# Splitting the stationary side of a Linformer-attention and hard-swish kernel into 64- and 32-column tiles

## Chip, cores, metric

One Trainium2 chip, one NeuronCore. The metric is the device time of one execution in microseconds (us); lower is better. L12 is a line of the kernel that a profile is of, so the same statement has other line numbers in the changed kernels (the layers: L497 and L532 before, L172 after).

## The reference

Attention with keys and values projected from 1024 to 64 positions, for 8 batches of 8 heads, then two layers with a hard-swish between:

```python
k_proj = np.einsum('ks,bhsd->bhkd', E, k)           # E, F: 64 x 1024
v_proj = np.einsum('ks,bhsd->bhkd', F, v)
scores = scale * np.matmul(q, k_proj.transpose(0, 1, 3, 2))
attn   = softmax(scores)
x      = np.matmul(attn, v_proj)                    # then to 8192 tokens x 512
h      = x @ w_in                                   # 512 x 2048
out    = (h * np.clip(h + 3.0, 0.0, 6.0) / 6.0) @ w_out
```

## The kernel before

Everything on TensorE is bf16 with f32 sums in PSUM. The layers of one batch run while the next batch's attention is slipped in between groups of them. Cut to what the change and the argument touch:

```python
def busy(n):                                        # warm-up of TensorE
    ps = pmm()
    for _ in range(n):
        nc.tensor.matmul(ps, ones[:, :P], ones, start=True, stop=True)
busy(12)
# ... projections: keys in columns 0..63, values in 64..127 (L195)
for so in range(SO):
    for e in range(2):
        nc.tensor.matmul(ps[e * KP:(e + 1) * KP], ef_t[e][:, so, :],
                         kqv[self.b]["kv"[e]][:, :, so, :], ...)
# ... then, for the batch after the next:
def turn(self):
    nc.sync.dma_start_transpose(self.kT, ...)       # keys turned by DMA
    ...
    qT_dma[self.b] = q_transposed(self.b)           # queries turned by DMA (batches 2 and 3: elsewhere)
    nc.gpsimd.tensor_copy(mark, last)               # waits for the last one turned
    load_kqv(self.b + 1, ...)                       # then the next batch's loads
# ... scores (L226), values (L244): 64 rows x 64 columns; sums (L264): 128 rows x 32 columns
# ... first layer (L497)
for ko in kos:
    nc.tensor.matmul(h_ps, w_in_sb[:, ko, fo * P:(fo + 1) * P], xT[:, ko, t, :], ...)
# ... second layer (L532)
for fo in range(FO):
    nc.tensor.matmul(o_ps, g[:, fo, c * P:(c + 1) * P], w_out_sb[:, fo, :], ...)
```

The chain in `turn`: the projection's keys go to SBUF, DMA turns them (kT), DMA turns the queries (qT), a one-element copy on GpSimd ("mark") waits for the last of these, and only then are the loads of the batch after issued, which the next projection needs. The queries of batches 2 and 3 are turned elsewhere; there "mark" waits for the keys.

The softmax here doesn't subtract the row's maximum and nothing guards it: scores larger than these inputs give would overflow.

Of the kernel before, what the change touches and what calls it, by code (L numbers as in the profile page):

```python
# [15 lines left out]
def kernel(  # L16
# [11 lines left out]
    nc = tc.nc  # L28
    B, H, S, D = q.shape
    KP = E.shape[0]  # L30
# [3 lines left out]
    P = 128  # L34
    SO = S // P
    KO = d_model // P
    FO = d_ff // P
# [28 lines left out]
    def pmm():  # L66
        return ps_mm.tile([P, TOK], f32, tag="mm", name="mm")

    def pat():
        return ps_at.tile([P, TOK], f32, tag="at", name="at")  # L70


    def g_tile():
        return gpool.tile([P, FO, TOK], bf16, tag="g", name="g")
# [12 lines left out]
    ident = consts.tile([P, P], bf16, name="ident")  # L87
# [9 lines left out]
    def raw_tile(name):  # L97
        return kqv_pool.tile([P, H, SO, D], bf16, tag=name, name=name)


    kqv = {0: {n: raw_tile(n) for n in ("k", "q", "v")}}
    q0 = kqv[0]["q"].rearrange("p h s d -> p (h s d)").rearrange(
        "p (t h s d) -> p t h s d", t=NB, h=H, s=SB)
# [22 lines left out]
    w_in_sb = consts.tile([P, KO, d_ff], bf16, name="w_in_sb")  # L126
    w_out_sb = consts.tile([P, FO, d_model], bf16, name="w_out_sb")
# [7 lines left out]
    for i in range(SB):  # L135
        c = slice(i * FO // SB, (i + 1) * FO // SB)
# [17 lines left out]
    ef_t = [e_t, f_t[:, :, 0, :]]  # L154
    busy(2)

    def q_transposed(b):

        t = qT_pool.tile([P, KO, 2, TOK], bf16, tag="qT", name="qT")
        nc.sync.dma_start_transpose(t.rearrange("p j a (m n) -> p (j a m) n", n=P),  # L160
                                    kqv[b]["q"].rearrange("p h s d -> p (h s d)"))
        return t

    qT_dma = {}

    def rec_tile():
        return att.tile([P, 2, TOK], f32, tag="rec", name="rec", bufs=4)

# [13 lines left out]
    class Attention:  # L182
# [8 lines left out]
        def project(self, alloc):  # L191
            ps = self.ps = alloc()
            for so in range(SO):
                for e in range(2):
                    nc.tensor.matmul(ps[e * KP:(e + 1) * KP], ef_t[e][:, so, :],  # L195
                                     kqv[self.b]["kv"[e]][:, :, so, :],
                                     start=(so == 0), stop=(so == SO - 1))

        def keys_out(self):
            for a in range(2):  # L200
# [116 lines left out]
        def visit(self, n, following):  # L317
# [3 lines left out]
            if n == 1:  # L321
                den, av = self.sums(0, pmm, pmm), self.values(0, pat, pat)
                last = self.scores(3, pat, pat)
                rec = rec_tile()
                inverse(rec, den)
                self.exps(3, last)
                return lambda: self.scaled(0, av, rec)
# [27 lines left out]
    class First:  # L355
# [31 lines left out]
        def queries(self, t, js):  # L387

            ps = pat().bitcast(bf16)[:, :len(js) * TOK]
            for i, j in enumerate(js):  # L390
                for a in range(2):
                    for m in range(2):
                        o = i * TOK + a * HT + m * P
                        nc.tensor.transpose(ps[:, o:o + P],  # L394
                                            q0[:, t, 2 * j + a, 2 * m:2 * m + 2, :].rearrange("p s d -> p (s d)"),
                                            ident)
            q = rec_tile().rearrange("p i n -> p (i n)").bitcast(bf16)[:, :2 * TOK]
            nc.vector.tensor_copy(q[:, :len(js) * TOK], ps)
            for i, j in enumerate(js):
                self.qT[t, j] = q[:, i * TOK:(i + 1) * TOK].rearrange("p (a n) -> p a n", a=2)  # L400
# [93 lines left out]

    def h_part(h_ps, xT, t, fo, kos):
        for ko in kos:
            nc.tensor.matmul(h_ps, w_in_sb[:, ko, fo * P:(fo + 1) * P], xT[:, ko, t, :],  # L497
                             start=(ko == 0), stop=(ko == KO - 1))

    def h_out(h_ps, g, fo):  # L500
        r = rpool.tile([P, TOK], f32, tag="r", name="r")
# [3 lines left out]
    def first_group(xT, t, g, fo):  # L505
        h_ps = pmm()
        h_part(h_ps, xT, t, fo, range(KO))
        h_out(h_ps, g, fo)

    def out_rows(b, t, c):  # L510
        return out_v[b, :, SB * t + 2 * (c % 2) + c // 2, :]


    def second_group(b, t, g, c, copy=None):
        o_dst = out_rows(b, t, c)
        if (b, t, c) == (B - 1, NB - 1, SB - 1):

            most = d_model * 3 // 4
            for piece, copy, dma in ((slice(0, most), nc.vector.tensor_copy, nc.sync),
                                     (slice(most, d_model), nc.scalar.copy, nc.scalar)):  # L520
                n = piece.stop - piece.start
                o_ps = pmm()[:, :n]
                for fo in range(FO):
                    nc.tensor.matmul(o_ps, g[:, fo, c * P:(c + 1) * P], w_out_sb[:, fo, piece],  # L524
                                     start=(fo == 0), stop=(fo == FO - 1))
                o_sb = opool.tile([P, d_model], f32, tag="o_sb", name="o_sb")[:, :n]
                copy(o_sb, o_ps)
                dma.dma_start(out=o_dst[:, piece], in_=o_sb)
            return
        o_ps = pmm()  # L530
        for fo in range(FO):
            nc.tensor.matmul(o_ps, g[:, fo, c * P:(c + 1) * P], w_out_sb[:, fo, :],  # L532
                             start=(fo == 0), stop=(fo == FO - 1))
            if fo % SB == SB - 1:
                yield
        o_sb = opool.tile([P, d_model], f32, tag="o_sb", name="o_sb")
        (copy or nc.scalar.copy)(o_sb, o_ps)  # L537
        nc.sync.dma_start(out=o_dst, in_=o_sb)

    def whole(gen):  # L540
        for _ in gen:
            pass

    def x_tile():
        return xpool.tile([P, KO, NB, TOK], bf16, tag="xT", name="xT")


    xT = x_tile()
    first = First(xT)
    g = [g_tile(), g_tile()]  # L550
# [41 lines left out]
    def pop():  # L592
        if later:
            later.pop(0)()
# [25 lines left out]
    xT = x_next  # L620
# [2 lines left out]

    second = Attention(2)
    for b in range(1, B):
        if b + 1 < B:
            x_next = second.xT = x_tile()
        third = Attention(b + 2) if b + 2 < B else None


        def visits(b, n):
            def nothing():
                pass

            if b == 1:
                n -= SB
                if n < 3:
                    return lambda: second.visit(n, third), nothing
                return nothing, lambda: second.visit(n, third)()
            if b + 1 < B:  # L640
                six = (pmm, pmm), (pat, pat), (pat, pat)
                if (b, n) == (2, 0):
                    return lambda: second.some_scores((2, 0, 1), six), nothing
                if (b, n) == (2, 1):
                    return lambda: second.some_scores((3,), six[1:2]), nothing
                if (b, n) == (2, 3):
                    return lambda: third.projected(pmm), nothing
                if n == 0:
                    return nothing, lambda: second.some_scores(
                        (1, 2, 3), ((pmm, pmm), (pat, pat), (pat, pmm)), third)  # L650
                if n == 2:
                    return second.sums_and_values, nothing
                if n == 5:
                    return second.first_products, nothing
                if n == 6:
                    return lambda: second.last_values(third), nothing
            return nothing, nothing

        for t in range(NB):
            if b == 1 and t == 1:  # L660
                qT_dma[3] = q_transposed(3)
            g = g_tile()
            for fo in range(FO):
                if b < 3 and t == 0 and fo < 2:

                    if fo == 0:
                        TwoGroups(xT, t, g).parts((0, 1, 2), (3,))
                else:
                    first_group(xT, t, g, fo)
                pop()  # L670
                if b == 1 and t == 0 and fo == 10:
                    second.projected()
                if not behind or fo % SB < SB - 1:
                    continue
                inside, after = visits(b, t * SB + fo // SB)
                rows = second_group(*behind[0], fo // SB, nc.vector.tensor_copy if b == 1 else None)
                next(rows)
                next(rows)
                rest = inside()
                whole(rows)  # L680
                after()
                if rest:
                    rest()
            behind = [(b, t, g)]
        second, xT = third, x_next
# [32 lines left out]
```

## Time and profile before

| | before |
|---|---|
| time, median of 6 runs | 507.32 us (507.19 to 507.92) |
| profiled span | 505.3 us |
| TensorE busy | 495.5 us (98%) |
| blocks of instructions fetched for TensorE | 21 |

The row of the instruction queue from the page's part on DMA queues (packets, MB, share of 16 engines):

```profile
q8 instruction: 21, 0.34, 0.3%
```

and two rows of DMA issues (count, median us from issue to landing):

```profile
kT<-kp SPq DMA_TRANSPOSE x7, 2.6
qT<-q SPq DMA_TRANSPOSE x7, 6.7
```

The timeline of before (start, length in us, engine, line) around the end of the chain in `turn`, for batch 3:

```profile
135.79 1.20 SPq L209 DMA_TRANSPOSE kT<-kp  x1
136.72 1.89 PE L532 MATMUL mm<-w_out_sb,g 128*128 128x512 bf16 x8
138.51 0.18 POOL L216 COPY mark<-kT 1x1 bf16<-1x1 bf16 x1 [35.30 <-DMA kT<-kp]
138.54 0.41 PE L226 MATMUL mm<-qT,kT 64*64 64x256 bf16 x8
```

The keys are turned at 138.51 and TensorE uses them at 138.54. TensorE does not wait, but it has next to nothing in hand: any delay of that DMA goes straight into the time.

### The profile page before, as it was taken

How to read it: one execution, taken by the hardware profiler on the slowest of the kernel's cores; microseconds unless marked ns; L12 is line 12 of the kernel's file. 1: busy time of each engine (PE TensorE's matmuls, PEld its weight loads, DVE VectorE, ACT ScalarE, POOL GpSimd, SP SyncE). 2: the span in 40 equal slices, each digit the busy share in tenths (PEclk: the TensorE clock that was granted, in tenths of full speed). 3: DMA queues.
4: the chain of work that ended last, by engine and by line, in shares of the span. 5: the costliest groups of instructions: out<-in, count | busy, mean ns of one | idle time of the engine just before them, and what ended most of it. 6: DMA issues, size and time to landing. Idle time of an engine off the chain costs nothing.

```text
span 505.3 us, 7033 instructions
## 1 busy us (share of the span) xinstructions
PE 495.5 (98%) x2728; PEld 224.9 (45%) x2778; DVE 245.3 (49%) x384; ACT 256.2 (51%) x438; POOL 38.7 (8%) x58
## 2 busy tenths in 40 slices
PE   8899999999999999999999999999999999999997
PEld 4444444444444444444444444444444444444444
DVE  3572736855733573526635455533752446334420
ACT  3757476567574444654555544654455544434431
POOL 8620020010020020010002000000000000000000
PEclk9999999999999999999999999999999999999999
DMA  9999989699199998699217990248110361101112
GB/s 168 198 205 208 195 154 231 123 162 204 61 159 198 260 153 161 137 169 257 98 43 134 215 263 28 62 97 209 42 43 30 82 162 43 40 24 42 43 42 83
DMA packets 78057, 66.02 MB, mean 131 GB/s; under 512 B 36216, under 2 KB 67192, under 8 KB 78024
## 3 DMA queue, kind: packets, MB, share of 16 engines
q0 software_dynamic: 32480, 29.36, 37.1%
q1 hardware_dynamic: 45320, 35.89, 27.1%
q8 instruction: 21, 0.34, 0.3%
q10 hardware_dynamic: 224, 0.33, 0.3%
q14 instruction: 12, 0.10, 0.1%
HBM read 69.73 MB, written 16.94 MB: 172 GB/s over the span
## 4 chain that ended last, share of the span: by engine, by line
PE 97%; ACT 1%; issue 1%; DVE 0%; ACTq 0%
PE mm L532 43%; PE mm L497 43%; PE at L195 2%; PE mm L93 1%; PE at L244 1%; PE at L226 1%; PE mm L244 1%; PE mm L524 1%; PE mm L264 1%; PE at L414 1%; ACT aT L235 0%; PE mm L226 0%; PE at L382 0%; PE at L394 0%; PE mm L195 0%
## 5 line engine op out<-in xcount | busy, mean ns | idle before, releaser
L503 DVE SCALAR_TENSOR_TENSOR g<-r,mm 128x512 bf16<-128x512 f32 x256 | 173.6, 687 | 178.9 <-ACT r L502 178.1
L497 PE MATMUL mm<-xT,w_in_sb 128*128 128x512 bf16 x997 | 229.0, 379 | 1.5
L532 PE MATMUL mm<-w_out_sb,g 128*128 128x512 bf16 x985 | 227.8, 379 | 1.9 <-issue 1.0
L502 ACT ACTIVATE r<-mm 128x512 f32<-128x512 f32 x256 | 152.3, 599 | 74.5 <-PE mm L497 73.2
L497 PEld LDWEIGHTS <-w_in_sb 128*128 128x128 bf16 x1024 | 99.5, 98 | 122.2 <-issue 3.3
L532 PEld LDWEIGHTS <-g 128*128 128x128 bf16 x1008 | 96.7, 98 | 120.6 <-issue 7.4
L537 ACT COPY o_sb<-mm 128x512 f32<-128x512 f32 x55 | 32.3, 587 | 126.6 <-PE mm L532 123.7
L257 DVE TENSOR_TENSOR xT<-at,rec 128x512 bf16<-128x512 f32 x42 | 26.5, 682 | 6.4 <-ACT rec L176 6.4
L235 ACT ACTIVATE aT<-at 128x512 bf16<-128x512 f32 x38 | 20.2, 615 | 9.1 <-PE at L226 9.1
L201 DVE CAST kp<-at 64x512 bf16<-64x512 f32 x12 | 7.7, 677 | 15.5 <-PE at L195 15.5
L216 POOL COPY mark<-qT 1x1 bf16<-1x1 bf16 x4 | 0.7, 176 | 161.9 <-DMA qT<-q 161.9
L235 ACT ACTIVATE aT<-mm 128x512 bf16<-128x512 f32 x18 | 10.3, 613 | 3.6 <-PE mm L226 3.6
L537 DVE COPY o_sb<-mm 128x512 f32<-128x512 f32 x8 | 5.5, 688 | 13.4 <-PE mm L532 13.4
L195 PE MATMUL at<-k,e_t 128*64 128x512 bf16 x48 | 11.5, 382 | 0.0
L195 PE MATMUL at<-v,f_t 128*64 128x512 bf16 x48 | 11.5, 381 | 0.0
L257 DVE TENSOR_TENSOR xT<-mm,rec 128x512 bf16<-128x512 f32 x14 | 9.0, 686 | 4.3 <-PE mm L244 4.3
L176 ACT ACTIVATE rec<-rec 128x1024 f32<-128x1024 f32 x10 | 10.6, 1060 | 0.3
L170 ACT ACTIVATE rec<-mm 128x512 f32<-128x512 f32 x10 | 5.5, 595 | 7.9 <-PE mm L244 5.4
L170 ACT ACTIVATE few<-mm 128x512 f32<-128x512 f32 x10 | 5.4, 595 | 7.4 <-PE mm L264 7.4
L93 PE MATMUL mm<-ones 128*128 128x512 bf16 x18 | 7.4, 549 | 1.5 <-DVE halves L84 1.5
L204 DVE CAST vp<-at 64x512 bf16<-64x512 f32 x12 | 8.3, 694 | 0.4
L195 PEld LDWEIGHTS <-e_t 128*64 128x64 bf16 x56 | 5.6, 109 | 6.2 <-issue 1.9
(75 smaller groups left out, 161.0 us busy)
## 6 DMA issues: line engine op xcount, KB each, us to landing
out_dram<-o_sb SPq DMA_DIRECT2D x63, 256.0 KB, 2.5
rec<-rows SPq DMA_DIRECT2D x40, 256.0 KB, 6.2
k<-in_k_dram POOLq DMA_DIRECT2D x7, 1024.0 KB, 14.1
v<-in_v_dram POOLq DMA_DIRECT2D x7, 1024.0 KB, 20.9
q<-in_q_dram POOLq DMA_DIRECT2D x7, 1024.0 KB, 10.7
w_out_sb<-in_moe_w_out_dram POOLq DMA_DIRECT2D x4, 512.0 KB, 16.3
w_in_sb<-in_moe_w_in_dram POOLq DMA_DIRECT2D x5, 256.0 KB, 9.8
k<-in_k_dram POOLq DMA_DIRECT2D x4, 256.0 KB, 5.6
```

Of the source, the lines that this page charges most:

```text
L93: nc.tensor.matmul(ps, ones[:, :P], ones, start=True, stop=True)
L170: nc.scalar.activation(rec[:, i], den, AF.Ln)
L176: nc.scalar.activation(flat, flat, AF.Exp, scale=-1.0)
L195: nc.tensor.matmul(ps[e * KP:(e + 1) * KP], ef_t[e][:, so, :], kqv[self.b]["kv"[e]][:, :, so, :], start=(so == 0), stop=(so == SO - 1))
L235: nc.scalar.activation(self.aT[j][:, r].rearrange("p a n -> p (a n)"), tiles[r], AF.Exp, scale=scale)
L244: nc.tensor.matmul(tiles[t][c:c + D].rearrange("p (r n) -> p r n", r=2), stationary(r, 2 * j + a), self.aT[j][r:r + KP, :, a, :], start=Tr ...
L257: nc.vector.tensor_mul(self.xT[:, j, t, :], av[t], rec[:, t])
L497: nc.tensor.matmul(h_ps, w_in_sb[:, ko, fo * P:(fo + 1) * P], xT[:, ko, t, :], start=(ko == 0), stop=(ko == KO - 1))
L502: nc.scalar.activation(r, h_ps, AF.Relu, bias=0.5, scale=1.0 / 6.0)
L503: nc.vector.scalar_tensor_tensor(g[:, fo, :], r, 1.0, h_ps, op0=ALU.min, op1=ALU.mult)
L532: nc.tensor.matmul(o_ps, g[:, fo, c * P:(c + 1) * P], w_out_sb[:, fo, :], start=(fo == 0), stop=(fo == FO - 1))
L537: (copy or nc.scalar.copy)(o_sb, o_ps)
```

## The change

The intent: a change of the array's tile shape (rows x columns in use by a matmul) costs TensorE about 0.1 us, as the prediction below reads from the trace, so give the layers, the projections and the transposes the column width of the small attention matmuls beside them: 64 columns at first, 32 (the width of the sums) from batch 2 on. A 128-column matmul becomes two or four that run side by side.

```diff
+    width = [P // 2]
+
+    def in_columns(ps, stationary, moving, **flags):
+        for lo in range(0, stationary.shape[-1], width[0]):
+            nc.tensor.matmul(ps[lo:lo + width[0]], stationary[:, lo:lo + width[0]], moving, **flags)
 ...                                   # projections, both layers, the split last rows, alike:
-            nc.tensor.matmul(h_ps, w_in_sb[:, ko, fo * P:(fo + 1) * P], xT[:, ko, t, :],
-                             start=(ko == 0), stop=(ko == KO - 1))
+            in_columns(h_ps, w_in_sb[:, ko, fo * P:(fo + 1) * P], xT[:, ko, t, :],
+                       start=(ko == 0), stop=(ko == KO - 1))
 ...                                   # transposes of batch 0's second half: two of 64 columns
     for b in range(1, B):
+        if b == 2:
+            width[0] = P // 4
```

More of the change, by code (lines that the diff above doesn't have):

```diff
@@ L194, in project @@
                 for e in range(2):
-                    nc.tensor.matmul(ps[e * KP:(e + 1) * KP], ef_t[e][:, so, :],
-                                     kqv[self.b]["kv"[e]][:, :, so, :],
-                                     start=(so == 0), stop=(so == SO - 1))
+                    in_columns(ps[e * KP:(e + 1) * KP], ef_t[e][:, so, :], kqv[self.b]["kv"[e]][:, :, so, :],
+                               start=(so == 0), stop=(so == SO - 1))
         def keys_out(self):
@@ L393, in queries @@
                         o = i * TOK + a * HT + m * P
-                        nc.tensor.transpose(ps[:, o:o + P],
-                                            q0[:, t, 2 * j + a, 2 * m:2 * m + 2, :].rearrange("p s d -> p (s d)"),
-                                            ident)
+                        n = width[0] if t else P
+                        for lo in range(0, P, n):
+                            nc.tensor.transpose(ps[lo:lo + n, o:o + P],
+                                                q0[:, t, 2 * j + a, 2 * m:2 * m + 2, :].rearrange(
+                                                    "p s d -> p (s d)")[:, lo:lo + n], ident)
             q = rec_tile().rearrange("p i n -> p (i n)").bitcast(bf16)[:, :2 * TOK]
@@ L523, in second_group @@
                 for fo in range(FO):
-                    nc.tensor.matmul(o_ps, g[:, fo, c * P:(c + 1) * P], w_out_sb[:, fo, piece],
-                                     start=(fo == 0), stop=(fo == FO - 1))
+                    in_columns(o_ps, g[:, fo, c * P:(c + 1) * P], w_out_sb[:, fo, piece],
+                               start=(fo == 0), stop=(fo == FO - 1))
                 o_sb = opool.tile([P, d_model], f32, tag="o_sb", name="o_sb")[:, :n]
@@ L531, in second_group @@
         for fo in range(FO):
-            nc.tensor.matmul(o_ps, g[:, fo, c * P:(c + 1) * P], w_out_sb[:, fo, :],
-                             start=(fo == 0), stop=(fo == FO - 1))
+            in_columns(o_ps, g[:, fo, c * P:(c + 1) * P], w_out_sb[:, fo, :],
+                       start=(fo == 0), stop=(fo == FO - 1))
             if fo % SB == SB - 1:
```

## The prediction

> **What bounds the kernel now.** I read the page first, for the share of each engine and the chain that ended last.
>
> ```profile
> PE 495.5 (98%) x2728; PEld 224.9 (45%) x2778; DVE 245.3 (49%) x384; ACT 256.2 (51%) x438; POOL 38.7 (8%) x58
> ...
> PEclk9999999999999999999999999999999999999999
> ...
> PE 97%; ACT 1%; issue 1%; DVE 0%; ACTq 0%
> PE mm L532 43%; PE mm L497 43%; PE at L195 2%; PE mm L93 1%; PE at L244 1%; PE at L226 1%; PE mm L244 1%; PE mm L524 1%; PE mm L264 1%; PE at L414 1%; ACT aT L235 0%; PE mm L226 0%; PE at L382 0%; PE at L394 0%; PE mm L195 0%
> ```
>
> TensorE is busy 98% of the span, the chain is TensorE for 97%, the clock is full everywhere, and VectorE and ScalarE stand at half. Two lines, the two layers (L497 and L532), are 86% of the chain. Busy is not peak, so next came the chain in order of time, where 16 matmuls of a layer always take the same time:
>
> ```profile
> 172.66 3.45 PE mm L497 x16
> ...
> 190.81 3.45 PE mm L532 x16
> ```
>
> 3.45 us / 16 = 216 ns for one 128x512 matmul. The 1024 matmuls of the first layer and the 1024 of the second (16 of them are split 384+128, which comes to the same) need 2048 x 0.216 = 442 us of the 505.3 us span. The view of waits holds only 4.5 us of idle TensorE in six rows, so no wait is there to be removed. What is left is how much a matmul costs beyond 216 ns. That is seen where the tile shape changes, in the timeline of TensorE:
>
> ```profile
> 152.72 1.24 PE L532 MATMUL mm<-w_out_sb,g 128*128 128x512 bf16 x5
> 153.89 0.61 PE L264 MATMUL mm<-aT,halves 128*32 128x512 bf16 x8
> 154.43 0.63 PE L244 MATMUL at<-aT,vp 64*64 64x512 bf16 x8
> 154.99 1.25 PE L532 MATMUL mm<-w_out_sb,g 128*128 128x512 bf16 x5
> ```
>
> The eight sums (128 rows x 32 columns) start at 153.89 and the values at 154.43. Eight 512-column matmuls in 0.54 us: four run side by side, two rounds of 0.216 = 0.43, and 0.11 is left over. The values to the next layer: 0.56 - 0.43 = 0.13 left over. In the trace's records the gap from the last start in one shape to the first in another is 309 to 312 ns wherever the earlier matmul has 512 columns, so 93 to 96 ns more than 216, and the second start after it is late by another 0 (32 columns), 10 (full), 14 (64x64) or 21 ns (128x64). The price is the same if only the columns change (L195 to L497: 311 ns), only the rows (L244 to L195: 306 ns), or both (L264 to L244: 309 ns).
>
> That narrow columns run side by side at full pace is seen at the projections, 64 columns each:
>
> ```profile
> 162.24 0.38 PE L195 MATMUL mm<-k,e_t 128*64 128x512 bf16 x1
> 162.25 0.38 PE L195 MATMUL mm<-v,f_t 128*64 128x512 bf16 x1
> 162.46 0.38 PE L195 MATMUL mm<-k,e_t 128*64 128x512 bf16 x1
> 162.46 0.38 PE L195 MATMUL mm<-v,f_t 128*64 128x512 bf16 x1
> ```
>
> A pair starts within 4 ns, and the next pair 216 ns later: two matmuls in the time of one.
>
> **What the Trainium skill says.** "TensorEngine Tiling (Array Packing)", Key Properties: a change of tiling mode drains TensorE, a change of tile within a mode does not. The trace agrees: about 93 ns at each change, nothing between L244 and L226, both 64x64. The same page, Restrictions: column tiling switches Fast Weight Load off. The trace shows no visible price so far: a load takes 98 ns at 128 columns, 106 to 110 at 64, 92 to 96 at 32, and they overlap. "TensorE: Matmul & The Clock Gate", the section on 56 ns against 53.3: N/2.4 + 2.5 ns per warm matmul (216 measured here at N=512), a floor of about 25 ns from start to start, and about 62 ns per matmul where the sequencer's microcode decodes it. No row of this trace decides which decoding is in force. "Runtime: NRT & Kernel Launch", Instruction fetch mechanics: instructions arrive in blocks of 16 KiB, 256 instructions, while the current ones run. The trace agrees: the instruction queue q8 has 21 packets and 0.34 MB, 16 KB each.
>
> **The change part by part.** No instruction of VectorE, ScalarE, GpSimd or a DMA changes; the order of the programs shows their counts equal. On TensorE a layer's matmul becomes two of 64 columns (batch 0 and 1) or four of 32 (from about 133 us on, some 370 us of the span); the rows of TensorE's program go from 5558 to 16310.
>
> Array time: unchanged. A group of two or four side by side takes 216 ns, as L195 and L264 do.
>
> Changes of shape: I counted them in the order of both programs, with the shapes that the groups by form give. Before: 100, of which 42 into the full shape, 11 into 128x64, 5 into 128x32, 38 into 64x64, the rest into 64x128. After: 87, of which 11 into full, 17 into 128x64, 17 into 128x32, again 38 into 64x64. The projections and the sums no longer stand apart, but scores and values keep 64 rows, so each visit to them still costs two changes. With 103 ns into full (93+10), 114 into 128x64 and 93 into 128x32: before 42x0.103 + 11x0.114 + 5x0.093 = 6.05 us, after 11x0.103 + 17x0.114 + 17x0.093 = 4.65 us. Gain 1.4 us.
>
> Small pieces: at the end, 16 matmuls of 128 columns (56 ns each now, in the records) become 16 groups of four, and their loads have no fast path. By the skill's columns/1.2 GHz the four loads need 4 x 27 = 107 ns if they queue behind each other: an estimate of up to 16 x 51 ns = 0.8 us, at the very end and on the path. The 16 transposes of batch 0's second half become pairs: up to the same again, 0.8 us. Half of each seems likely, because 64-wide loads at L366 already keep 56 ns: 0.8 us together.
>
> Sum: -1.4 + 0.8 = -0.6 us, and the time goes from 507.3 to about 506.7.
>
> **The rivals.** (1) Issue becomes the bound. Four loads and four matmuls in 216 ns allow 27 ns per instruction; today two share 216. For it: the skill's 62 ns under microcode would make a group at least 4 x 62 = 248 ns, some 1650 groups x 32 ns = +53 us, about 560; if the loads cost the same, 496 ns a group, over 960 us. Against: the records show starts 3 to 4 ns apart, and the 24 scores at 321.24 with their 24 loads go through in 0.6 us, 12 ns per instruction, without a hole. But 48 is fewer than the 64 instructions that the skill gives TensorE's queue, so a burst does not prove a sustained rate. I give it 12%.
>
> (2) Instruction fetch. 16310 rows are 64 blocks, one per 32 groups = 6.9 us in the later part against one per some 24 us now. q8's 0.3% of 16 engines x 505 us is 24 us, 1.15 us a block: enough room when nothing is in the way. While the loads of the next batch fill the DMA engines (99% in many slices up to 240 us) a block can start late, and TensorE could starve for some us a few times: +2 to +15 us. I give it 15%.
>
> (3) A gain larger than the count of changes, over 2% = 10 us. It would need 100 changes removed, all there are, or a group faster than 216 ns; nothing in the trace offers either. 1%.
>
> **Range and chances.** The main case, some 75%, lies between 505 and 508.5 (1.4 us of gain, up to 1.6 us of loss at the small pieces, and drift). Fetch stalls stretch it to about 522; issue as the bound lies beyond. The range that should hold 8 in 10 is 504.5 to 525. Faster by over 2% (below 497.2): 0.01. Slower by over 2% (above 517.5): 0.19, the issue rival and a part of the fetch rival. Within: 0.80. Predicted 506.7.
>
> **What would show it.** Right, if in the changed profile 16 groups of four still take 3.45 us in the chain, the gap at changes stays near 310 ns, and layers to sums and to projections have no such gap from batch 2 on. The small pieces at the end then take longer than 16 x 56 ns. Wrong, if groups of four start more than 216 ns apart in a steady stretch (issue), the more so at 32 than at 64 columns; or if idle stretches of a us or more appear on TensorE put down to "issue", thick while DMA is busy and gone after 400 us (fetch); or if rows of TensorE wait for PSUM buffers that were free before.

## The result, and the profile after

| | before | after |
|---|---|---|
| time, median of 6 runs | 507.32 us (507.19 to 507.92) | 508.41 us (507.50 to 509.98) |
| ratio | 1 | 1.0023 (95%: 1.0007 to 1.0039) |
| profiled span | 505.3 us | 507.0 us |
| TensorE matmuls, counted by their weight loads (50 matmul records are missing before) | 2778 | 8154 |
| blocks of instructions | 21 | 63 |

Ratios here and below are the mean time of one kernel's fast runs over that of the other's in the same rounds, so not quite the ratio of the medians. The result lies in the predicted range and within 2%, but on the other side of before than predicted: 1.1 us slower, where 0.6 us faster was expected. The page's rows of the engines and of the instruction queue:

```profile
PE 498.1 (98%) x8154; PEld 249.3 (49%) x8154; DVE 245.2 (48%) x384; ACT 256.4 (51%) x438; POOL 38.7 (8%) x58
...
q8 instruction: 63, 1.03, 0.8%
```

The chain in order of time shows what a group of four now takes:

```profile
219.25 27.74 PE mm L172 x512
```

27.74 us / 128 groups is 217 ns, and in the trace's records the group starts are 216 ns apart, as one full matmul's were. Eight instructions per 216 ns are no strain. The timeline at the sums, which the prediction showed for before:

```profile
153.90 1.90 PE L172 MATMUL mm<-w_out_sb,g 128*32 128x512 bf16 x32
155.63 0.60 PE L271 MATMUL mm<-aT,halves 128*32 128x512 bf16 x8
156.16 0.63 PE L251 MATMUL at<-aT,vp 64*64 64x512 bf16 x8
156.72 1.05 PE L172 MATMUL mm<-w_out_sb,g 128*32 128x512 bf16 x16
```

From the layer to the sums it is 1.73 us = 8 x 0.216: the gap is gone there, and those before and after the values (64x64) are still there. So the intended effect took place. What is new stands in TensorE's waits (total us, times, longest):

```profile
PE mm L233 <- DMA kT<-kp: 1.3, 1, 1.3
PE at L172 <- DMA v<-in_v_dram: 0.9, 2, 0.5
...
PE mm L233 <- DMA qT<-q: 0.2, 1, 0.2
```

Before had no row of TensorE waiting for a DMA. Two more such rows, left out here (batch 0's values 0.6 us, its keys 0.5), lie in the first 20 us, where before waited for other engines instead; the table below starts after them, with a lag of 0.12 us. To see when the time came and went, I paired the 384 instructions of VectorE, which are the same in both kernels, and took how much later each one ends in the changed kernel:

| stretch of the kernel before | lag at its start, us | lag at its end, us | what happens |
|---|---|---|---|
| 54 to 59 | 0.12 | 0.59 | projection waits for batch 1's values; two changes of shape fewer |
| 67 to 76 | 0.58 | 0.79 | scores wait for turned queries |
| 94 to 99 | 0.82 | 0.59 | two changes of shape fewer |
| 136 to 144 | 0.63 | 2.03 | scores wait for turned keys (kT) |
| 144 to 198 | 2.03 | 1.53 | 0.17 back at once, in the scores after the wait (0.78 us in place of 0.98); then three changes of shape fewer |
| 198 to 208 | 1.53 | 2.28 | projection waits for batch 5's values; one change of shape fewer |
| 208 to 502 | 2.28 | 1.71 | six changes of shape fewer |

The losses are 0.5 + 0.2 + 1.4 + 0.75 = 2.8 us, the gains 0.2 + 0.5 + 0.6 = 1.3 us. Of the gains 0.2 us is the time made good right after the keys' wait, whose net cost is so 1.2 us; the other 1.1 us belongs to 11 changes of shape (counted in the order of the weight loads: 100 before, 87 after), 0.1 us each. (The recorded texts speak of batch 4's values at 203 and 204 us; what the turn of batch 4 loads are the values of batch 5.) The largest loss, in the timeline that was shown for before:

```profile
136.43 1.20 SPq L216 DMA_TRANSPOSE kT<-kp  x1
137.35 1.90 PE L172 MATMUL mm<-w_out_sb,g 128*32 128x512 bf16 x32
140.57 0.41 PE L233 MATMUL mm<-qT,kT 64*64 64x256 bf16 x8 [1.31 <-DMA kT<-kp]
140.65 0.18 POOL L223 COPY mark<-kT 1x1 bf16<-1x1 bf16 x1 [36.74 <-DMA kT<-kp]
```

From the issue of the transpose to the first scores: 4.14 us, against 2.75 before. The records of single DMA packets in the trace show why. The transpose's packets run from 137.6 to 138.6, but two of its 32 closing packets of 4 bytes start only at 139.48 and 139.49; at 138.41 a 16 KB packet of the instruction queue starts, and it takes 1.09 us, to 139.50. The trace does not name the engine of a packet; that two packets of 32, one sixteenth, start when the block ends fits one of the 16 engines being held. (The last packet is about 0.9 us late, the scores 1.4 us; "mark" follows the last packet after 1.15 us in place of 0.59, and the records do not show why.) In the kernel before the transpose's last packet starts by 138.0, and the instruction packet comes at 139.37, after it. This gave the theory.

**Theory F**: a block of 256 instructions arrives as one packet of 16 KB, which holds one of the 16 DMA engines for about 1 us. A transfer with packets on that engine ends that much later. Narrow tiles make TensorE's program three times as long (63 blocks in place of 21), so more transfers are hit, and those with no time in hand make TensorE wait. **Rival S**: a moving operand that is read once per column tile slows DMA in SBUF. **Rival C**: chance in DMA times.

### The profile page after: what moved, and what is told of

It reads as the page before. It is cut to its first block, busy times and chain, and to the rows that moved or that the text cites. A ratio compares the mean times of both kernels' runs of the same rounds, so it can differ in the third digit from the quotient of the medians.

```text
span 507.0 us, 17834 instructions
## 1 busy us (share of the span) xinstructions
PE 498.1 (98%) x8154; PEld 249.3 (49%) x8154; DVE 245.2 (48%) x384; ACT 256.4 (51%) x438; POOL 38.7 (8%) x58
## 4 chain that ended last, share of the span: by engine, by line
PE 76%; DMA 18%; POOL 2%; ACT 1%; issue 1%; DVE 1%; SPq 1%; POOLq 0%; ACTq 0%
PE mm L172 71%; DMA q<-in_q_dram 6%; DMA v<-in_v_dram 6%; DMA qT<-q 4%; DMA w_in_sb<-in_moe_w_in_dram 2%; PE at L172 1%; PE at L251 1%; DMA kT<-kp 1%; PE mm L251 1%; PE at L233 1%; POOL q L106 1%; POOL k L110 1%; ACT aT L242 0%; PE mm L271 0%; POOL v L110 0%
## 5 line engine op out<-in xcount | busy, mean ns | idle before, releaser
L172 PE MATMUL mm<-w_out_sb,g 128*32 128x512 bf16 (+3 forms) x3776 | 235.6, 376 | 0.2 <-DVE g L512 0.2
L172 PE MATMUL mm<-xT,w_in_sb 128*32 128x512 bf16 (+1 forms) x3584 | 232.2, 379 | 0.2 <-ACT aT L242 0.2
L172 PEld LDWEIGHTS <-w_in_sb 128*32 128x32 bf16 (+1 forms) x3584 | 112.4, 99 | 108.9 <-issue 1.3
L172 PEld LDWEIGHTS <-g 128*32 128x32 bf16 (+1 forms) x3776 | 110.9, 98 | 110.8 <-issue 7.0
L172 PE MATMUL at<-v,f_t 128*32 128x512 bf16 (+1 forms) x72 | 11.4, 380 | 0.9 <-DMA v<-in_v_dram 0.9
L172 PE MATMUL at<-k,e_t 128*32 128x512 bf16 (+1 forms) x72 | 11.8, 381 | 0.0
L233 PEld LDWEIGHTS <-kT 64*64 64x64 bf16 x224 | 5.6, 106 | 6.2 <-issue 3.2
```

The lines of the kernel that those rows point to most:

```text
L172: nc.tensor.matmul(ps[lo:lo + width[0]], stationary[:, lo:lo + width[0]], moving, **flags)
L233: nc.tensor.matmul(tiles[r][t * KP:(t + 1) * KP, a * HT:(a + 1) * HT], self.kT[r * D:(r + 1) * D, 2 * j + a, :], qT[r * D:(r + 1) * D, j, ...
```

## The experiments

Nine kernels ran, all with correct results, each with five rounds against the kernel before.

**e1, 64 columns to the end.** Half as many extra instructions.

```diff
-        if b == 2:
-            width[0] = P // 4
```

> All tiled matmuls 64 columns wide, to the end. Read from the two profiles: the narrow tiles themselves cost nothing (a group takes 216 ns), the changed kernel gains about 0.1 us at each change of shape that is gone (1.4 us), and loses 2.8 us in four waits of TensorE for DMA (0.5 us at 55.6, 0.2 at 69, 1.4 at 140.6, 0.75 at 204.3). Theory F (instruction blocks): the instruction queue's 16 KB packet holds one DMA engine for about 1 us, and a transfer with packets on that engine ends that much later; with narrow tiles there are 63 such packets in place of 21. Here the program has 9718 rows, 38 blocks, and the changes of shape fall from 100 to 91, worth 0.7 us. The first 133 us are the changed kernel's own, so the waits at 55.6 and 69 should be there again, those at 140.6 and 204.3 may be gone or shorter: time 506.7 to 508, fewer waits than in the changed kernel. Rival S (the array reads the moving operand once per column tile, and that slows DMA in SBUF): half the reads of 32 columns, so waits about half as long everywhere, none gone. Rival C (chance: DMA time varies by run): waits anywhere, times spread like the changed kernel's, 507.5 to 510.

507.17 us (506.90 to 507.92), 0.9996 of before (0.9984 to 1.0008). The waits at 55.6, 140.6 and 204.3 are gone; one of 0.4 us for turned queries is left:

```profile
PE mm L233 <- DMA qT<-q: 0.4, 1, 0.4
```

Two tenths of a us for weights come at 20 as well. This fits F and C. The wait at 55.6 had been expected again, since the program up to there is the changed kernel's own, and it did not come: that one is not tied to the tiles.

**e2, 32 columns from the start.**

```diff
-    width = [P // 2]
+    width = [P // 4]
     ...
-        if b == 2:
-            width[0] = P // 4
```

> All tiled matmuls 32 columns wide from the start; 18262 rows, 71 blocks, changes of shape 86, worth 1.8 us against before. Theory F: blocks come every 6.9 us in the first 133 us too, where the loads of the first batches fill the DMA engines, so new or longer waits for DMA there: the sum of TensorE's waits for DMA 2 to 5 us, time 507.5 to 511, slower than the changed kernel by some 0 to 2 us. Rival S: waits in the first 133 us twice as long as in the changed kernel (0.7 to 1.4 us). Rival C: same as the changed kernel.

508.03 us (507.39 to 510.68), 1.0018 of before (1.0001 to 1.0036); waits of 0.6 us for weights at 20, 0.5 us at the scores at 69 and 0.5 us for the values of batch 5 at 203. Not worse than the changed kernel, so the number of blocks alone does not set the time. On S this run says little: the waits at 20 and 69 add up to 1.1 us, within its 0.7 to 1.4, but the one at 55 is gone.

**e3, the changed kernel with its blocks shifted.** The 12 warm-up matmuls are cut in four: 72 instructions more and the same work, so each block is fetched 72 instructions earlier.

```diff
-    busy(12)
+    busy(12, 4)        # 48 matmuls of 128 columns in place of 12 of 512
```

> The changed kernel with its 12 warm-up matmuls of 512 columns cut into 48 of 128: same time of TensorE while it is waiting for its first data anyway, but 72 instructions more ahead of everything, so every block of 256 instructions is fetched 72 instructions earlier: 1.9 us earlier where tiles have 32 columns, 3.9 us where they have 64. Nothing else changes: the tiles, their reads and their changes of shape are those of the changed kernel. Theory F: the fetch at 138.4 us in the changed profile, which lies on the transpose of the keys (packets 137.6 to 139.5), moves to about 136.5 and leaves it free, so the wait of 1.4 us at 140.6 goes; that at 55.6 is likely to go too (its fetch at 54.9 moves to 51). Time 505.5 to 507, faster than the changed kernel by 1 to 2.5 us and perhaps than the kernel before. Rivals S and C: no change, 507.5 to 510.

508.52 us (508.24 to 511.01), 1.0029 of before (1.0014 to 1.0043). The time is not what F expected, but the named wait is gone:

```profile
137.04 1.90 PE L172 MATMUL mm<-w_out_sb,g 128*32 128x512 bf16 x32
138.87 0.41 PE L233 MATMUL mm<-qT,kT 64*64 64x256 bf16 x8
```

The block is fetched at 135.85, ahead of the transpose's packets, and the scores start 2.76 us after its issue, as in the kernel before. The wait at 69 is gone too, that at 55 was to go and shrank to 0.3 us. The gain was lost again at 203, where the wait for batch 5's values grew:

```profile
PE at L172 <- DMA v<-in_v_dram: 1.2, 1, 1.2
```

That wait ends the chain of `turn`: the transpose of batch 4's queries is issued at 169 us, and the loads follow it. In e3 two blocks fall on that transpose, at 172.6 (a packet of 2.08 us this time) and 178.7. The times of all kernels, the ones below included, put the stretch from the issue of that transpose to the mark that waits for it beside the blocks fetched in it:

| kernel | blocks in the stretch | issue to mark, us | loads of batch 5 end at, us |
|---|---|---|---|
| before | 0 | 8.3 | 198.4 |
| e4, e5, e7 | 0 | 8.8, 8.8, 8.7 | 200.5, 200.9, 199.1 |
| e1, e6, e8, e9 | 1 | 9.3, 9.0, 10.1, 10.1 | 201.2, 200.7, 201.1, 201.6 |
| e2, e3, after | 2 | 10.9, 11.7, 10.9 | 202.6, 203.1, 203.9 |

Against the mean of the four without one (8.65 us), one block goes with 0.3 to 1.4 us more and two with 2.2 to 3.0. The projection wants the values at about 202, so none or one block is covered and two are not. With 32 columns a block is due every 6.9 us (32 groups x 216 ns), shorter than the transpose, so no shift can keep every block out of it. This table alone does not tell F from S: the three kernels with two blocks are also the three with 32 columns at that time. Other transposes do; see the end of this section.

**e4, full tiles up to batch 3, 32 columns from batch 4 on.**

```diff
-    width = [P // 2]
+    width = [P]
-        if b == 2:
+        if b == 4:
     ...
-        for lo in range(0, stationary.shape[-1], width[0]):
+        n = min(width[0], stationary.shape[-1])
+        for lo in range(0, stationary.shape[-1], n):        # and n for width[0] in the slices
```

> Full 128-column tiles up to batch 3's layers, 32 columns from batch 4 on (from about 254 us): the early part, where the loads of the next batch are tight, has the instruction rate of the kernel before. Changes of shape 96, worth 0.5 us. Theory F and theory S both: no waits for DMA in the first 254 us, time 506.6 to 507.0, that is 0.5 us faster than before. Rival C: spread as in the changed kernel. If it is slower than before, the narrow tiles cost something of their own in the steady part that the comparison of the two profiles did not show.

507.88 us (507.56 to 508.71), 1.0009 of before (0.9996 to 1.0022): not the gain that both theories expected. Nor did it run without waits for DMA: batch 1's values cost 0.5 us at 55, with full tiles. The narrow tiles then won back 0.36 us, so that the last copy on VectorE ends only 0.07 us later than before's, but the span is 1.0 us longer. What is lost besides lies after the last copy of ScalarE:

```profile
502.40 0.27 ACT L537 COPY o_sb<-mm 128x128 f32<-128x128 f32 x1 [2.91 <-PE mm L173]
502.70 0.35 ACTq L538 DMA_DIRECT2D out_dram<-o_sb  x1
```

In the packet records the last packets of the two last stores start at 504.56 and 504.76 (in the kernel before, after the same copy at 502.33, at 503.50 and 503.84), and a block of instructions was fetched from 502.65 to 503.71, on top of the stores. F's mechanism at a place that I had not thought of; a mere reading so far, tested by e7.

**e5, the kernel before with 32 instructions more.** Full tiles; the warm-up is cut into 28 shorter matmuls of the same total length.

```diff
-    busy(12)
+    busy(4)
+    busy(4, 2)
+    busy(4, 4)
```

> The kernel before, with full tiles, its 12 warm-up matmuls cut into 28 shorter ones of the same total length: 32 instructions of TensorE more, no work more. The program then ends just past a boundary of 256 instructions, as late32's did (12246 rows, 5590 here: both 42 short of a multiple of 256 in the rows that the listing counts), whose block was fetched at 502.65 to 503.71, on the last stores of the output. Theory F (instruction blocks hold up a DMA engine): a 22nd block is fetched at about 502.6, the last stores land about 0.9 us later, time 508.2, 0.9 us slower than before, though no tile changed. Theory S (the reads of narrow tiles slow DMA) and rival C (chance): no change, 507.2 to 507.6. If the block is not fetched at the end, the run tells nothing on F.

508.46 us (508.39 to 508.70), 1.0021 of before (1.0009 to 1.0034): 0.96 us slower, the size expected, and not where it was expected. The last block was fetched at 499.0 and met nothing. It was the keys' transpose again that was hit:

```profile
136.87 1.89 PE L534 MATMUL mm<-w_out_sb,g 128*128 128x512 bf16 x8
140.14 0.41 PE L228 MATMUL mm<-qT,kT 64*64 64x256 bf16 x8 [1.39 <-DMA kT<-kp]
```

A block is fetched at 138.08 and takes 0.93 us. The transpose's packets, which began at 137.1, end with two stragglers at 139.00 and 139.01, where the block ends, and the scores start 4.21 us after the issue, as in the changed kernel (4.14). So the very wait that cost the changed kernel 1.4 us comes about in the kernel before, without one narrow tile, by moving its block fetches. Rival S cannot do that, and rival C would have to hit all five runs here and spare all five of e6 below.

**e6, the kernel before with 72 instructions more**, the control: `busy(12, 4)` as in e3.

> Control for the two shifts: the kernel before with the warm-up cut into 48 matmuls of 128 columns, 72 instructions more. The last boundary comes 40 instructions earlier than in e5, so its block is fetched about 2 us earlier, ahead of the last stores. Theory F: 507.2 to 507.8, with no wait at the end; a collision elsewhere would show as a wait for DMA beside a fetch. If cutting the warm-up itself costs time, it shows here.

507.43 us (507.33 to 507.51), 1.0000 of before (0.9988 to 1.0013). The block comes at 133.0, well ahead of the transpose, and the scores start 2.75 us after its issue. Cutting the warm-up shows no cost. A wait of about 0.4 us for batch 1's values at 55.3 shows here too, with full tiles: this wait of the changed kernel is not due to the change, or not only.

**e7, e4 with 72 instructions more**: `busy(12, 4)` again.

> late32 (full tiles up to batch 3, 32 columns from batch 4 on) with the warm-up cut into 48, 72 instructions more. In e4 the layers ended only 0.07 us later than in the kernel before and the whole 1.0 us later, because the last block was fetched on top of the last stores. Here that fetch comes about 1 us earlier. Theory F: the end is free again, time 506.8 to 507.2, 0.7 to 1 us faster than e4 and 0.3 to 0.6 faster than before. If the end is late again though the fetch is away from it, F is wrong about the end.

507.10 us (506.73 to 507.58), 0.9994 of before (0.9982 to 1.0007), 0.8 us faster than e4 by the medians; the two ran in different rounds and their intervals overlap, so the profile has to decide. There the last block is fetched at 501.75, about 0.9 us earlier, the last packet of the output starts 1.51 us after the last copy starts, as in before (2.36 in e4), and the span ends no later after the last copies than before's. This run met the wait at 55 as well (0.7 us), and even so is not slower than before.

**e8 and e9, 64 columns at first, 32 from batch 4 or from batch 3 on.** e4 with `width = [P // 2]`, and e9 with `b == 3`.

> 64 columns up to batch 3's layers (e1's, which met one wait of 0.4 us at 68), 32 from batch 4 on; 14198 rows, the last boundary far from the end. Changes of shape 89, worth 1.06 us. Theory F: no wait at 140 or 204 (at most one fetch in the transpose of batch 4's queries, as in e1), no late end: time 506.3 to 507.0, the best of all, if no new collision appears. Theory S: as e1 in the first half, and no more than 0.4 us better than e1.

> e8 with the change to 32 columns one batch earlier, from batch 3 on (about 194 us), after the transpose of batch 4's queries at 168 to 178 is over. Changes of shape 88 in place of 89, worth another 0.15 us; 60 blocks. Theory F: no block in that transpose more than e8 has, so no wait at 204, time 506.2 to 507.0, as e8 or 0.15 us better; if a block now falls on the landing of batch 4's values at about 200, a wait of up to 0.9 us at 204 comes back and the time is 507.0 to 508. Rival S: narrow tiles from 194 on slow the loads of batch 4 that run until 200, wait at 204 as in the changed kernel (0.75 us) whatever the blocks do.

e8: 507.06 us (506.67 to 507.75), 0.9994 of before (0.9980 to 1.0008). e9: 507.00 us (506.71 to 508.12), 0.9996 (0.9983 to 1.0008). Neither has a wait at 140 or 204, though e9's tiles have 32 columns while the loads of batch 5 run until 201.6: against S. Both wait for turned queries at 69, 0.2 and 0.5 us, which their expectations had left out. By the medians these are the fastest, 0.4 us ahead of before (507.42 to 507.50 in these rounds), but the intervals hold 1. No version is shown to be faster than the kernel before; for four with narrow tiles (e1, e7, e8, e9) no loss is shown either.

**All transposes beside the blocks.** The eleven traces hold many more transposes of the same sizes, which separate the width of the tiles from the blocks. From issue to landing (where the view gives no landing, to 0.12 us before "mark"), in us; those of batch 4's queries are in the table above:

| transpose | block starts after its issue by | full tiles | 64 columns | 32 columns |
|---|---|---|---|---|
| keys | no block starts in it | 2.57 to 2.73 (18) | 2.57 to 2.73 (11) | 2.60 to 2.61 (4) |
| keys | 1.98 to 2.15 | 4.16 (e5) | 4.14 (e3, batch 2) | 4.10 (after) |
| queries | no block starts in it | 6.6 to 6.7 (15) | 6.7 (8) | none |
| queries | 0.1 to 1.1 | 6.7 (2) | 6.7 (1) | 6.7 to 7.5 (4) |
| queries | 6.1 to 6.6 | 8.2 to 8.4 (3) | 8.3 to 8.5 (5) | 8.2 to 8.4 (10) |

Those left out have a block elsewhere and lie between these values, except one with two blocks (e2, 9.74). One with 32 columns and a block at 6.12 (e2) took 6.66, so not every late block does harm. Without a block the width makes no difference, while with one at the same place full tiles lose as much as narrow ones: S is out as the cause of these delays, and the place of the block counts, not only its presence. This settles the wait at 69 as well: in the changed kernel, e1, e2, e8 and e9 a block starts 6.2 to 6.6 us after the issue of batch 1's queries and TensorE waits; the other six have no block there and do not, e3 with the changed kernel's own tiles among them.

## Why the prediction was right, and where it was not

- **Array time unchanged at 216 ns a group**: right, for two tiles of 64 columns and for four of 32.
- **Gain of 1.4 us at the changes of shape**: right. The 11 that the table of lags shows by themselves are worth 1.1 us, 0.1 us each, so the 13 some 1.3 (an estimate from these). The gap is a little less uniform than the prediction read it: 306 to 312 ns in before's layers, up to 333 in the work of batch 0, 305 to 320 in the changed kernel. And the six rows of TensorE's idle time, which the prediction put at 4.5 us, add up to 4.1.
- **Small pieces, +0.8 us**: wrong, nothing was lost. In the changed kernel's records the last 16 groups of four matmuls of 128 moving columns start 56 ns apart, as one full matmul did before, and so do the pairs of narrow transposes. The step that failed is the four narrow loads queueing behind each other for 107 ns: the whole group, loads included, took 56 ns.
- **Rival 1, issue**: did not occur, and could be dropped: eight instructions per 216 ns in steady stretches, and eight per 56 ns at the end. That is 14 ns a matmul, below the floor of 25 ns from start to start that the prediction took from the skill.
- **Rival 2, instruction fetch**: the right cause of loss, and the wrong path. I had TensorE starve for instructions; it never did. The blocks delayed other DMAs, and TensorE waited for their data: a term of +2.8 us in the profiled run that the main sum did not have. Of it the 1.4 us for the turned keys are shown to come from a block (e3 takes the wait away, e5 makes it with full tiles), the 0.2 us at 69 go with a block late in the queries' transpose (six kernels without one have no wait, e3 among them), and the 0.75 us for batch 5's values are supported by the two tables of transposes, not shown by a run of their own. The 0.5 us at 55.6 occur with full tiles as well (e4, e6, e7) and are not due to the change alone.
- **Sum**: -0.6 us was forecast and +1.1 us measured. With the terms as the profiled run shows them: -1.3 (the gains of the table) + 0 (small pieces) + 2.8 (waits for DMA), which with some 0.1 us at the start is the 1.7 us between the two profiled spans. That 508.41 lies even in the main case's 505 to 508.5 is luck: its upper end was meant for the small pieces, which cost nothing, and the waits for DMA that filled it were in no term. The wider range had been left open for the fetch, on another path and for 2 to 15 us.

The changed kernel also scatters more: 507.5 to 509.98 against 507.19 to 507.92. With more waits open to DMA times that is to be expected, but no run took it apart.

## What to carry to other kernels

Splitting a full matmul into column tiles was free for the array here (216 ns a group at 512 moving columns, 56 ns at 128) and saved about 0.1 us at each change of shape that it removed, so count those changes first: here 13 of 100. It also multiplies the instructions, and each block of 256 is a packet of about 1 us in DMA; a DMA that TensorE waits for with nothing in hand (keys turned at 138.51, used at 138.54) can lose more by one such packet than the tiles gain. Where the times of two versions differ by a microsecond, shift the blocks with a few harmless instructions before believing in either cause: 32 of them cost the untouched kernel 0.96 us.

## What the Trainium skill lacked or had wrong

- "Runtime: NRT & Kernel Launch", Instruction fetch mechanics, calls the cost of a block boundary mostly hidden. It lacks that the block's packet takes 0.88 to 2.08 us (the median of each kernel is 0.95 to 1.08) and that other transfers are held up by it: 1.4 us at the keys' transpose, about 1.6 us late in a queries' transpose (8.2 to 8.5 us in place of 6.7), 0.9 us at the last stores (e4).
- "TensorEngine Tiling (Array Packing)", Key Properties, gives no price for the drain at a change of mode: some 90 to 105 ns to the first start in the layers (305 to 320 ns in place of 216, both kernels) and 0 to 21 ns at the second, alike for rows, columns or both.
- The same page, Restrictions, has column tiling without Fast Weight Load, and "TensorE: Matmul & The Clock Gate", LDWEIGHTS, gives columns/1.2 GHz, from which I estimated 107 ns for four loads: four loads and four matmuls of 128 moving columns took 56 ns a group.
- "TensorE: Matmul & The Clock Gate", Back-to-back issue gap, gives about 131 ns sustained per matmul at N=512 and 81 ns at N=128 for pairs of load and matmul; these runs show 216 ns and 56 ns (sixteen in a row at the end of before).
- No page gives TensorE's sustained rate of issue for narrow tiles: at least eight instructions per 216 ns over hundreds of groups (512 matmuls in 27.74 us), and eight per 56 ns over 16 groups.
